# One TensorE program of FFT mixing and sorted experts: its order made by a count of every instruction

## The chip, the core and the metric

The kernel runs on one core of a Trainium2 chip. A core has a matrix engine (TensorE, PE in the profile; its weight loads are PEld), a vector engine (VectorE, DVE), a scalar engine (ScalarE, ACT), a general engine (GpSimd, POOL) and a queue processor that starts transfers (SyncE, SP). Each works through its own list of instructions in order and waits on semaphores for the others. Sixteen DMA engines move data. The metric is the time of one execution on the device in microseconds; the median of a few runs is compared.

## What is computed

The input `x` is 8 x 2496 x 256. Each channel of each batch goes through a Fourier transform along the sequence, a product with a learned filter, and the inverse transform. The result, seen as 19968 rows of 256, goes through a mixture of eight experts in which each row takes the one expert of largest logit.

```python
def _attn_ref(x, filt_r, filt_i):
    X = np.fft.rfft(x, axis=1)
    F = (filt_r + 1j * filt_i)[None, :, :]
    return np.fft.irfft(X * F, n=x.shape[1], axis=1).astype(np.float32)

def _moe_ref(x, w_gate, w1, w2):            # x (19968, 256), E = 8, F = 1024
    logits = x @ w_gate
    expert_idx = np.argmax(logits, axis=1)
    ...                                     # gate_w: softmax value of that expert
    for e in range(E):
        lo, hi = boundaries[e], boundaries[e + 1]      # rows sorted by expert
        h = np.maximum(x_sorted[lo:hi] @ w1[e], 0.0)
        y_sorted[lo:hi] = h @ w2[e]
    y = y_sorted[inv_perm]
    return gate_w[:, None] * y
```

## The kernel before

**The Fourier part.** 2496 is 39 x 64, and the transform is done in two short ones. For each batch: stage A multiplies blocks of `x` by the 39-point table (`tas`, L363), copies the result out of PSUM and stores it to DRAM (`zd`); stage B loads it the other way round (`fin<-zd`), multiplies by the 64-point table (`tbs`, L377), and VectorE multiplies by the filter in three instructions (L384 to L386) and adds two halves (on GpSimd in L390 or on VectorE in L393); stage C multiplies by the inverse table (`tcs`, L403), and its result is stored (`ud`); stage D loads that and multiplies by the last table (`tds`, L424). Batch 0 does the two turns in SBUF with transposes instead of DRAM (`first_a`, `turn_z`, `first_c`, `turn_u`). After stage D the rows are transposed, the logits are multiplied out (`logits` and `turn_logits` for batches 0 to 2, `block_logits` and `block_back` from batch 3), and `route` works out the expert and the row's place in the sorted list. GpSimd then scatters the rows to DRAM (`rows`, L693).

**The experts.** Sorted rows are read back in tiles of 512, 256 or 128 (`xg`), transposed on VectorE (L826), and multiplied by half of an expert's first weights at a time (`w1t`). Large tiles use a product of seven instead of eight blocks (`hidden_by_quarters`): GpSimd makes sums of blocks of `x` and `w1` (`sums`, `wsum`), VectorE adds the products together (L873), ScalarE takes the Relu (L877). Then each group of 128 rows is multiplied by the second weights (`w2t`, eight instructions of 128x256, L927), scaled by its gate (L931 or L932), and scattered to the output by GpSimd (L933).

**What sets the order.** The lists of TensorE, VectorE, ScalarE and SyncE are in the order in which the Python program emits instructions; GpSimd's list is arranged by the framework. The program keeps a list of Fourier steps, `STEPS`, sorted by hand-given places, each a tuple of place, function, load that it needs, assumed TensorE time, and chain ("a", "b", "d", "l"). A generator `experts()` yields the experts' pieces in their order. The main loop picks a Fourier step or an expert piece. It goes by a rough clock, `now[0]`, which grows by the assumed time of each step emitted, and by `free`, which holds rough times at which VectorE, ScalarE and GpSimd are done. A load is taken to land 7 to 13 us after it was asked for:

```python
lands[kind, b, c] = now[0] + (13.0 if kind != "x" and c < 2 else 10.0)
```

A step whose load is taken to be late is put off for another of the next sixteen; the steps that need another engine's output are placed by their place in the list alone. `credit` and `share()` mix expert pieces into the Fourier steps by the ratio of work left. `either` puts a copy out of PSUM on VectorE or ScalarE, whichever `free` says is done first.

Stores are kept in `moves` and issued by `flush` one round of the loop after they were asked for. `more_loads` asks for the next loads into seven `fin` buffers, and for `z` and `u` only after the stores of the whole batch are issued (`stored`). `prefetch` asks for rows and weights of coming expert tiles. `side` advances `route` by small pieces.

Of the kernel before, what the change touches and what calls it, by code (L numbers as in the profile page):

```python
# [19 lines left out]
P = 128  # L20
# [103 lines left out]

@with_exitstack
def kernel(
# [16 lines left out]
    nc = tc.nc  # L143
    mm = nc.tensor.matmul
    B = x.shape[0]
# [18 lines left out]
    dram = ctx.enter_context(tc.tile_pool(name="dram", bufs=1, space=DRAM))  # L164
# [7 lines left out]
    perm = ctx.enter_context(tc.tile_pool(name="perm", bufs=1))  # L172
# [9 lines left out]
    ps = ctx.enter_context(tc.tile_pool(name="ps", bufs=7, space=PSUM))  # L182

    fft = ctx.enter_context(ExitStack())
    cst = fft.enter_context(tc.tile_pool(name="cst", bufs=1))
    sb = fft.enter_context(tc.tile_pool(name="sb", bufs=2))
    psr = fft.enter_context(tc.tile_pool(name="psr", bufs=1, space=PSUM))
# [25 lines left out]
    pro = first.enter_context(tc.tile_pool(name="pro", bufs=2, side="right"))  # L213
# [4 lines left out]
    def experts_pool():  # L218
        first.close()
        pools["moe"] = ctx.enter_context(tc.tile_pool(name="moe", bufs=2, side="right", reuse_waits="tile"))  # L220
# [5 lines left out]
    now = [0.0]  # L226
    free = {"v": 0.0, "s": 0.0, "p": 0.0}

    def either(n, on_vector, on_scalar):

        v = max(free["v"], now[0]) + 0.15 + n / 960
        s = max(free["s"], now[0]) + 0.16 + n / 1200
        if v <= s:
            free["v"] = v
            on_vector()
        else:
            free["s"] = s
            on_scalar()

    def evac(o, i, n):  # L240
        either(n, lambda: nc.vector.tensor_copy(o, i), lambda: nc.scalar.copy(out=o, in_=i))

    def pool(start, n):

        free["p"] = max(free["p"], start) + 1.3 * n
        return free["p"]
# [36 lines left out]
    def make_constants():  # L283
        make_identity(nc, ident)
# [31 lines left out]
    ins, outs, lgs, yts, lands = {}, {}, {}, {}, {}  # L316
    NIN, YB = 7, 6

    moves, stored = [[], []], set()

    def move(o, i):
        moves[1].append(lambda: nc.sync.dma_start(out=o, in_=i))

    def mark(key):
        moves[1].append(lambda: stored.add(key))

    def flush(everything=False):
        for k in range(2 if everything else 1):
            for m in moves[k]:
                m()  # L330
        moves[:] = [[], []] if everything else [moves[1], []]
# [38 lines left out]
    def stage_b(b, f):  # L370
# [16 lines left out]
        free["v"] = max(free["v"], now[0]) + 2.1  # L387

        if b == 0 or b < 3 and not sides:
            nc.gpsimd.tensor_tensor(ys, ys, yw, op=ALU.add)  # L390
            free["p"] = max(free["p"], free["v"]) + (1.4 if b else 0.0)
        else:
            nc.vector.tensor_tensor(ys, ys, yw, op=ALU.add)  # L393
            free["v"] += 0.7
# [60 lines left out]
    def turn_z(f):  # L455
        if f % 4 == 0:
            nc.scalar.copy(out=ht[HP:, f:f + 4], in_=ht[:HP, f:f + 4])
            free["s"] = max(free["s"], now[0]) + 1.1
# [7 lines left out]
    def first_c(f):  # L466
# [6 lines left out]
        for h in range(DH):  # L473
            evac(zu["u"][:, h, :, :, f:f + 2], p[:, h].rearrange("p i c t -> p t c i"), D)

# [17 lines left out]
    def turn_y(b, c):  # L493
# [3 lines left out]
        if by_blocks(b):  # L497
# [3 lines left out]
            free["v"] = max(free["v"], now[0]) + 0.1 + n * D / 960  # L501
# [10 lines left out]

    turned_at = {}

    def turn_block(b, c):
        turn_y(b, c)
        turned_at["t", b, c] = max(now[0] + 4.0, free["v"] + 2.0)
# [4 lines left out]
    def block_logits(b, c):  # L522
# [10 lines left out]
        turned_at["s", b, c] = max(now[0], free["v"], free["s"]) + 1.5  # L533
# [35 lines left out]
    def route(b, c0, c1):  # L569
# [37 lines left out]
        due = free["v"] + 1.0  # L607
        while now[0] < due:
            yield "wait"
# [9 lines left out]
        free["s"] = max(free["s"], now[0]) + 1.2  # L619
# [15 lines left out]
        if by_blocks(b):  # L635
# [6 lines left out]
            due = free["v"] + 1.0  # L642
            while now[0] < due:
                yield "wait"
# [7 lines left out]
            free["s"] = max(free["s"], now[0]) + 0.3  # L652
# [12 lines left out]
        free["p"] = max(free["p"], now[0]) + 0.5 * len(yos)  # L665
        rows = []
        for t in range(w):
            m = N1 if t0 + t == NG - 1 else TP
            rows.append((row[:m, t:t + 1], yos[t // 4][:m, t % 4, :]))
        pool(now[0] + 2.0, 0)  # L670
        for t, (at, what) in enumerate(rows):
            scatter(b, at, what)
            yield "pool"
            if t % 4 == 3 or t == w - 1:
                held_y[0] -= 1
        if t0 + w == NG:
            rows_at[b] = free["p"] + 4.0
# [14 lines left out]
    def scatter(key, at, what):  # L692
# [11 lines left out]
        pool(now[0], 1)  # L704
# [117 lines left out]
    def turn_x(i):  # L822
# [4 lines left out]
        free["v"] = max(free["v"], now[0]) + DH * (0.15 + n * P / 960)  # L827
        if quarters(i):

            b = xts[i][:, :, :n * P].rearrange("p h (r c) -> p h r c", r=2)  # L830
            t = sums[i] = pools["moe"].tile([P, 3, 2 * P], F32, tag="sums", name="sums", bufs=2)[:, :, :n * HP]
            nc.gpsimd.tensor_tensor(t[:, 0], b[:, 0, 1], b[:, 0, 0], op=ALU.subtract)
            nc.gpsimd.tensor_tensor(t[:, 1], b[:, 1, 1], t[:, 0], op=ALU.subtract)

            nc.gpsimd.tensor_tensor(b[:, 0, 1], b[:, 1, 1], b[:, 0, 1], op=ALU.subtract)
            nc.gpsimd.tensor_tensor(t[:, 2], b[:, 1, 0], t[:, 1], op=ALU.subtract)
            free["p"] = max(free["p"], free["v"]) + 0.75 * n
            when["sums", i] = free["p"] + 1.0

    def w1_sums(h):  # L840

        w = w1t[h]
        t = wsum[h] = pools["moe"].tile([P, 3, 2 * P], F32, tag="wsum", name="wsum", bufs=2)
        nc.gpsimd.tensor_tensor(t[:, 0], w[:, 0, 1], w[:, 1, 1], op=ALU.add)  # L844
        nc.gpsimd.tensor_tensor(t[:, 1], t[:, 0], w[:, 0, 0], op=ALU.subtract)  # L845

        nc.gpsimd.tensor_tensor(w[:, 0, 1], w[:, 0, 0], w[:, 0, 1], op=ALU.subtract)
        nc.gpsimd.tensor_tensor(t[:, 2], w[:, 1, 0], t[:, 1], op=ALU.subtract)
        free["p"] = max(free["p"], now[0]) + 3.0
        when["wsum", h] = free["p"] + 1.0  # L850

    def hidden_by_quarters(h):
# [6 lines left out]
        w, ws, t = w1t[h], wsum[h], sums[i]  # L859
# [12 lines left out]
        def add(o, q, a):  # L872
            nc.vector.tensor_tensor(o, q, a, op=ALU.add)  # L873
            free["v"] = max(free["v"], now[0], free["s"] if o is first else 0.0) + 0.15 + 0.14 * n

        def relu(o, q):
            nc.scalar.activation(o.rearrange("p v r c -> p v (r c)"), q.rearrange("p v r c -> p v (r c)"), AF.Relu)  # L877
            free["s"] = max(free["s"], now[0], free["v"]) + 0.2 + 0.22 * n
# [4 lines left out]
        free["s"] = max(free["s"], now[0]) + 0.6  # L883
# [3 lines left out]
        q = product(ws[:, 1], t[:, 1])  # L887
# [4 lines left out]
        q = product(ws[:, 0], t[:, 0])  # L892
        add(hT[:, 1, :, 1], q, low)
        add(part, q, part)
        q = product(w[:, 1, 1], t[:, 2])
# [8 lines left out]
    def hidden(i, g, a):  # L904
# [10 lines left out]
        either(m, lambda: nc.vector.tensor_scalar_max(hT, p[:, :m], 0.0),  # L915
               lambda: nc.scalar.activation(hT, p[:, :m], AF.Relu))  # L916

    def result(i, j):
# [11 lines left out]
        pool(now[0], 1)  # L930
        either(D, lambda: nc.vector.tensor_scalar(ys, in0=p[:, :D], scalar1=gate, scalar2=None, op0=ALU.mult),  # L931
# [13 lines left out]
    def slot(k):  # L945

        steps, nch = [], len(CH)
        if k == 0:
            steps.append((0.4, load_rest, None, 0.0, None))
            for f in range(-2, NF + 2, 2):  # L950
                at = (f + 2) / (NF + 4)
                if 0 <= f < NF:
                    steps.append((at, lambda f=f: stage_b(k, f), None, 0.85, "b"))
                if f + 2 < NF:
                    steps.append((at + 0.01, lambda f=f: turn_z(f + 2), None, 0.44, "b"))
                if f >= 2:
                    steps.append((at + 0.02, lambda f=f: first_c(f - 2), None, 0.85, "b"))
        elif k < B:
            for f in range(0, NF + 4, 2):
                at = f / (NF + 4)  # L960
                if f < NF:
                    steps.append((at, lambda f=f: stage_b(k, f), ("z", k, f // 4) if f % 4 == 0 else None, 0.85, "b"))
                if f >= 4:
                    steps.append((at + 0.01, lambda f=f: stage_c(k, f - 4), None, 0.85, "b"))
# [277 lines left out]
```

## Time and profile before

| What | Value |
|---|---|
| Median of three runs | 1531.31 us (1528.97 to 1533.0) |
| The profiled execution | 1526.13 us, its span 1524.1 us |
| Mean granted TensorE clock | 0.992 |
| TensorE busy | 1458.8 us |
| VectorE, ScalarE, GpSimd busy | 769.3, 474.0, 698.2 us |
| Transfers | 276.89 MB, mean 182 GB/s |

In the profile a row of a group names line, engine, operation and tiles (output<-inputs), how often it ran, its busy time and the mean time of one. A row of waits names the engine and line that waited, what released it, and the total, number and longest of these waits in microseconds. A row of a stretch gives, after its bounds and length, the busy time and number of instructions of each engine, the granted clock as a share of full speed, the mean share of time in which the DMA engines were busy, and the GB/s moved. An SPq row is the queue processor's own wait or issue. A matrix instruction in fp32 leaves two records on PE.

### The profile page before, as it was taken

The page shows a single profiled execution, that of the slowest core. Times are in us where ns is not written, and L with a number is a line of the kernel's source. Part 1 is how long each engine was busy: PE and PEld are TensorE (multiplying, and loading weights), DVE is VectorE, ACT ScalarE, POOL GpSimd, SP SyncE. Part 2 cuts the span into 40 slices and gives each one's busy share as a digit, 9 for nine tenths or more (in the row PEclk, how much of TensorE's full clock was granted, in tenths as well). Part 3 has the DMA queues.
Part 4 walks back from the last instruction along what each step waited for, and adds up shares of the span by engine and source line. Part 5 has one row for each costly group of instructions (what it writes and reads, how often), then busy time and mean ns, then how long its engine had stood idle before and what let it go on. Part 6 is the DMA issues. An engine that isn't in the chain of part 4 may idle for free. (4 is left out here: it accounts for less than half of the span.)

```text
span 1524.1 us, 24305 instructions
## 1 busy us (share of the span) xinstructions
PE 1458.8 (96%) x7392; PEld 1147.9 (75%) x7392; DVE 769.3 (50%) x1712; ACT 474.0 (31%) x1003; POOL 698.2 (46%) x924
## 2 busy tenths in 40 slices
PE   7988897999988999999999999998999999999998
PEld 6543554776755866777778778887888889999997
DVE  4677585316665556567666565455525343440000
ACT  3444351233233233322232322222222222224332
POOL 4243334415523655545464556663545555741111
PEclk9999999999999999999999999999999999999999
DMA  9669898796479648657543744544566453455661
GB/s 241 196 180 313 250 321 244 213 250 224 135 208 273 182 129 251 186 170 186 172 133 112 210 113 126 159 132 128 163 169 192 142 175 102 123 185 170 185 186 39
DMA packets 216276, 276.89 MB, mean 182 GB/s; under 512 B 125209, under 2 KB 163610, under 8 KB 216147
## 3 DMA queue, kind: packets, MB, share of 16 engines
q1 hardware_dynamic: 197027, 231.99, 53.7%
q0 software_dynamic: 19120, 43.33, 8.3%
q8 instruction: 62, 1.02, 0.3%
q14 instruction: 67, 0.55, 0.1%
HBM read 195.24 MB, written 80.64 MB: 181 GB/s over the span
## 5 line engine op out<-in xcount | busy, mean ns | idle before, releaser
L927 PE MATMUL bank<-w2t,hT 128*128 128x256 f32 x1984 | 446.0, 383 | 8.3 <-ACT hT L877 7.8
L873 DVE TENSOR_TENSOR hT<-bank,hT 128x512 f32<-128x512 f32 (+1 forms) x504 | 298.7, 626 | 280.0 <-PE bank L869 188.0
L927 PEld LDWEIGHTS bank<-w2t,hT 128*128 128x128 f32 x1984 | 377.5, 191 | 70.6 <-issue 8.8
L933 POOL DMA_INDIRECT out_dram<-ys,ng x161 | 160.2, 995 | 451.2 <-ACT ys L932 111.7
L877 ACT ACTIVATE hT<-hT 128x1024 f32<-128x1024 f32 (+1 forms) x144 | 131.7, 955 | 345.4 <-DVE hT L873 345.2
L693 POOL DMA_INDIRECT rows<-yo,row x176 | 177.8, 1010 | 64.1 <-issue 44.2
L869 PE MATMUL bank<-xT,w1t 128*128 128x256 f32 (+1 forms) x864 | 191.6, 358 | 0.9 <-DVE yw L386 0.7
L932 ACT ACTIVATE ys<-bank,ng 128x256 f32<-128x256 f32 x135 | 63.8, 473 | 393.6 <-PE bank L927 325.8
L869 PEld LDWEIGHTS bank<-xT,w1t 128*128 128x128 f32 x864 | 152.2, 191 | 24.9 <-issue 5.7
L869 PE MATMUL bank<-sums,wsum 128*128 128x256 f32 (+1 forms) x576 | 137.3, 361 | 8.8 <-POOL wsum L845 4.3
L927 PE MATMUL bank<-w2s,hT 128*128 x592 | 132.6, 379 | 0.0
L826 DVE STREAM_TRANSPOSE xT<-xg 128x512 f32<-128x512 f32 (+2 forms) x126 | 57.4, 493 | 145.7 <-PE bank L910 119.6
L910 PE MATMUL bank<-xT,w1t 128*128 128x128 f32 (+1 forms) x864 | 123.4, 299 | 2.2 <-DVE xT L826 1.9
L869 PEld LDWEIGHTS bank<-sums,wsum 128*128 128x128 f32 x576 | 101.0, 191 | 28.8 <-issue 11.3
L910 PEld LDWEIGHTS bank<-xT,w1t 128*128 128x128 f32 x864 | 114.2, 191 | 11.1 <-issue 5.2
L927 PEld LDWEIGHTS bank<-w2s,hT 128*128 128x128 f32 x592 | 110.3, 190 | 13.8
L844 POOL TENSOR_TENSOR wsum<-w1t 128x256 f32<-128x256 f32 x72 | 52.9, 734 | 68.1 <-PE bank L869 65.9
L384 DVE TENSOR_TENSOR ys<-bank,ht 128x512 f32<-128x512 f32 x80 | 54.9, 687 | 55.5 <-PE bank L377 55.1
L403 PE MATMUL bank<-ys,tcs 128*128 128x512 f32 x140 | 73.7, 613 | 7.5 <-DVE ys L393 4.9
L363 PE MATMUL bank<-fin,tas 117*120 117x512 f32 x154 | 75.6, 610 | 5.4 <-DMA fin<-in_x_dram 4.5
L916 ACT ACTIVATE hT<-bank 128x128 f32<-128x128 f32 (+1 forms) x207 | 61.8, 299 | 48.1 <-PE bank L910 43.0
L377 PE MATMUL bank<-fin,tbs 128*128 128x512 f32 x140 | 72.6, 605 | 3.1 <-DMA fin<-zd 1.8
(160 smaller groups left out, 1602.1 us busy)
## 6 DMA issues: line engine op xcount, KB each, us to landing
w1t<-in_moe_w_dram SPq DMA_DIRECT2D x126, 512.0 KB
w2t<-in_moe_w_dram SPq DMA_DIRECT2D x68, 512.0 KB
fin<-in_x_dram SPq DMA_DIRECT2D x39, 512.0 KB
fin<-zd SPq DMA_DIRECT2D x70, 256.0 KB
ud<-uo SPq DMA_DIRECT2D x70, 256.0 KB
zd<-zo SPq DMA_DIRECT2D x35, 480.0 KB
fin<-ud SPq DMA_DIRECT2D x35, 480.0 KB
xg<-rows SPq DMA_DIRECT2D x112, 128.0 KB
```

The lines of the kernel that those rows point to most:

```text
L363: mm(p[:TK, :], lhsT=tas, rhs=xt[:TP, j:j + 2, :], start=True, stop=True)
L377: mm(p, lhsT=tbs, rhs=zi[:, j:j + 2, :], start=True, stop=True)
L403: mm(p, lhsT=tcs, rhs=ys, start=True, stop=True)
L693: sc = nc.gpsimd.indirect_dma_start(out=rowsd, out_offset=bass.IndirectOffsetOnAxis(ap=at, axis=0), in_=what, in_offset=None,)
L869: mm(q[:, v], lhsT=left[:, v * P:(v + 1) * P], rhs=right, start=True, stop=True)
L873: nc.vector.tensor_tensor(o, q, a, op=ALU.add)
L877: nc.scalar.activation(o.rearrange("p v r c -> p v (r c)"), q.rearrange("p v r c -> p v (r c)"), AF.Relu)
L910: mm(p[:, :m], lhsT=w1t[2 * i + g][:, dh, fh, v * P:(v + 1) * P], rhs=xts[i][:, dh, :m], start=(dh == 0), stop=(dh == DH - 1))
L916: lambda: nc.scalar.activation(hT, p[:, :m], AF.Relu))
L927: mm(p[:, :D], lhsT=hs[i][k % 4 // 2][:, k // 4, k % 2, j * P:(j + 1) * P], rhs=w2, start=(k == 0), stop=(k == FT - 1))
L932: lambda: nc.scalar.activation(ys, p[:, :D], AF.Copy, scale=gate))
L933: nc.gpsimd.indirect_dma_start(out=out, out_offset=bass.IndirectOffsetOnAxis(ap=gis[i].bitcast(U32)[:, j, :1], axis=0), in_=ys, in_offset= ...
```

## The change

The assumed times of steps and loads are replaced by a count. A class `Order` stands in front of the framework's engines. Every instruction that the program emits goes through it and is given a start: the latest of its engine's time, the counted end of its operands, and the counted release of the buffer that it writes (its last user `n` buffers ago). Its duration comes from a formula by engine and size. Transfers go through one counted stream. Matrix instructions that start over 1.2 us after the last one ended are counted at double time for 3.4 us.

```diff
+class Order:
+    HOP = 0.1
+    LOAD = 2.0
...
+    def transfer(self, out, in_):
+        n = min(self.run(out), self.run(in_), 4096)
+        packet = float(np.interp(n, (32, 64, 256, 1024, 4096), (9, 11, 18, 46, 159)))
+        size = 4 * int(np.prod([d[1] for d in in_.ap]))
+        return size / n * packet / 16e3
+
+    def count(self, engine, op, args, named):
...
+        kept = [a for a in ins if a.space != DRAM or a.name[:2] in ("zd", "ud")]
+        free = self.t[engine]
+        start = max([free] + [self.done.get(a.name, 0.0) + (self.HOP if engine != "sync" else 0.0) for a in kept])
+        if out is not None:
+            start = max(start, self.ahead.pop(out.name, 0.0))
...
+        if op.endswith("dma_start"):
+            busy = 1.0 if engine == "gpsimd" else 0.4
+            self.t[engine] = start + busy
+            took = self.transfer(out, named["in_"])
+            self.t["transfers"] = max(self.t["transfers"], start + busy) + took
+            end, tail = self.t["transfers"], self.LOAD
+        else:
...
+            elif engine == "tensor":
+                if start > self.busy + 1.2:
+                    self.slow = start + 3.4
+                rows = out.ap[0][1]
+                took = max(0.1, 0.00085 * n) if op == "transpose" else max(0.216, 0.00169 * n) if rows > 32 else 0.00045 * n
+                took *= 2.0 if start < self.slow else 1.0
+                tail = 0.25
+            elif engine == "vector":
+                took = 0.15 + n / 960
+            elif engine == "scalar":
+                took = 0.16 + n / 1200
+            else:
+                took = 0.06 + n / 375
```

`either` now also looks at the counted end of its input. The add of stage B goes to GpSimd when that is counted to cost little, not by batch:

```diff
-        if b == 0 or b < 3 and not sides:
+        if max(t["gpsimd"], t["vector"]) + 1.43 <= t["vector"] + (1.5 if b < 3 else 0.7):
             nc.gpsimd.tensor_tensor(ys, ys, yw, op=ALU.add)
         else:
             nc.vector.tensor_tensor(ys, ys, yw, op=ALU.add)
```

Stores go, in order, when their source is counted ready:

```diff
-    def flush(everything=False):
-        for k in range(2 if everything else 1):
-            for m in moves[k]:
-                m()
-        moves[:] = [[], []] if everything else [moves[1], []]
+    def flush():
+        while moves and (moves[0][0] is None or nc.ready(moves[0][0]) <= t["tensor"] + 0.2):
+            moves.pop(0)[1]()
```

Each Fourier step gains a sixth entry, the tiles that it reads; `turn_block` and the chain of `turned_at` go, and their steps read `yts` and `outs["s", ...]` in the same way. Two examples:

```diff
-                    steps.append((at, lambda f=f: stage_b(k, f), None, 0.85, "b"))
+                    steps.append((at, lambda f=f: stage_b(k, f), None, 0.85, "b", lambda f=f: [outs["zi", f]]))
...
-                    steps.append((at, lambda c=c: stage_d(k - 1, c), ("u", k - 1, c) if k > 1 else "y", 0.43 * CH[c][1], "d"))
+                    steps.append((at, lambda c=c: stage_d(k - 1, c), ("u", k - 1, c) if k > 1 else "y", 0.43 * CH[c][1], "d",
+                                  lambda c=c: [ins["u", k - 1, c] if k > 1 else outs["ui", c]]))
```

For an expert piece `when` gives the counted time of its tiles: rows, weights, sums, or the hidden layer and second weights. The main loop takes the first candidate that is counted ready within 0.2 us; when none is, it moves TensorE's counted time on:

```diff
+            steps = list(open_steps())
+            choice = [(f, wait_of(f)) for f in steps]
+            if known:
+                late_by = max(0.0, when(e[2]) - t["tensor"])
+                choice.insert(0 if credit > 0.0 or not fs else 1, (e, late_by))
+            choice = [c for c in choice if c[1] is not None]
+            pick, late_by = next((c for c in choice if c[1] <= 0.2), min(choice, key=lambda c: c[1]) if choice else (None, 0.5))
+            if late_by > 0.2:
+                t["tensor"] += min(late_by, 0.5)
+            elif pick is e:
                 e[0]()
-                now[0] += e[1]
                 credit -= e[1]
                 e = next(es, None)
-            elif f and ready(fs[n]):
-                f = fs.pop(n)
-                f[1]()
-                now[0] += f[3]
-                credit = (credit if asked else 0.0) + share() * f[3]
-                left_t[0] -= f[3]
             else:
-                now[0] += 1.0
+                fs.remove(pick)
+                pick[1]()
+                credit = (credit if known else 0.0) + share() * pick[3]
+                left_t[0] -= pick[3]
```

`open_steps` gives the first step of each chain among the next sixteen. The same clock replaces `now[0]` in `prefetch`, `side`, `route` and `due`. Arithmetic, tiles, buffers and the loads' sizes are as before.

## What was predicted before the changed kernel ran

> **What bounds the kernel now.** I read the page's busy times first, then the stretches of 100 us, then TensorE's waits, then the SP queue's waits, and last two places in the timeline.
>
> ```profile
> span 1524.1 us, 24305 instructions
> PE 1458.8 (96%) x7392; PEld 1147.9 (75%) x7392; DVE 769.3 (50%) x1712; ACT 474.0 (31%) x1003; POOL 698.2 (46%) x924
> ```
>
> TensorE is busy for 96% of the span, and the change neither adds nor removes a matmul. All it can win is TensorE's idle time, 1524.1 - 1458.8 = 65.3 us, and time at a lowered clock. The stretches (PE, PEld, DVE, ACT, POOL busy, then granted clock, DMA share, GB/s) say where that lies:
>
> ```profile
> 0.00:100.00 100.00, 86.92 (x440) 56.33 (x441) 57.23 (x109) 44.31 (x87) 37.86 (x57) 1.00 0.74 202
> 100.00:200.00 100.00, 88.65 (x329) 46.45 (x328) 66.36 (x167) 38.45 (x90) 39.35 (x49) 0.98 0.88 280
> 200.00:300.00 100.00, 87.24 (x372) 57.73 (x371) 60.28 (x181) 33.06 (x76) 41.08 (x58) 0.97 0.86 258
> 300.00:400.00 100.00, 99.88 (x485) 74.27 (x486) 44.07 (x97) 32.08 (x74) 40.65 (x54) 1.00 0.75 221
> 400.00:500.00 100.00, 91.46 (x420) 63.36 (x411) 59.30 (x133) 31.27 (x62) 39.07 (x53) 0.97 0.75 204
> 500.00:600.00 100.00, 95.69 (x454) 71.45 (x453) 60.28 (x117) 30.88 (x58) 57.81 (x76) 0.98 0.67 197
> 1000.00:1100.00 100.00, 96.14 (x444) 83.70 (x443) 52.45 (x120) 23.93 (x34) 51.01 (x67) 1.00 0.50 148
> ```
>
> Idle: 13.1 us in the first 100, 11.4 + 12.8 = 24.1 in the next 200, about 21.4 from 300 to 1100 (0.1, 8.5, 4.3, and 8.5 after 600), nothing from 1100 to 1500, 6.5 at the end. The clock shares 0.98, 0.97, 0.97, 0.98 are 2 + 3 + 3 + 2 = 10 us lost at half clock, half of it before 300. From 100 to 300 the transfers are the second limit: share 0.88 and 0.86.
>
> ```profile
> PE bank L927 <- ACT hT L877: 7.8, 2, 4.3
> PE bank L869 <- DVE hT L873: 5.9, 5, 2.0
> PE bank L446 <- DMA fin<-in_x_dram: 5.1, 2, 4.2
> PE bank L403 <- DVE ys L393: 4.9, 3, 1.7
> PE bank L363 <- DMA fin<-in_x_dram: 4.5, 2, 3.9
> PE bank L869 <- POOL wsum L845: 4.3, 1, 4.3
> ```
>
> Each row is who waited, who released it, total us, times, longest. Most are matmuls put too close behind the engine that makes their operand; two rows are loads.
>
> ```profile
> 441.04 2.00 ACT L877 ACTIVATE hT<-hT 128x1024 f32<-128x1024 f32 x2 [4.34 <-DVE hT L873]
> 443.09 3.15 PE L927 MATMUL bank<-w2t,hT 128*128 128x256 f32 x7 [4.27 <-ACT hT L877]
> ```
>
> Here a result matmul stands right behind the last product of its hidden layer; the Relu ends 4.27 us later. With other work in between that wait is gone: this is what the change is about.
>
> **The change, part by part.** I weigh the order of TensorE's instructions, before and after, by the spacing of matmul starts in this trace (0.43 us for a 128x256 instruction, which is two records, 0.86 for 512 columns, 0.11 for a transpose); the whole order is 1412 us of such work in both. For each operand I then count the work between the matmul it descends from and the matmul that uses it.
>
> 1. *Pieces go when counted ready.* Distances that were zero or short grow: Relu output to first result matmul, shortest three 0.9, 4.0, 4.3 before and 4.0, 6.7, 6.9 after; `zi` to stage B, 0.0 before and 0.9 after; `ui` to stage D, 0.0 and 0.9; route's `oe` to its two matmuls, under 3 us in 7 of 24 cases before and 3 after. Operands used under 0.6 us after their engine's last matmul, whatever the engine: 12 before, 3 after. One grows worse: block_back's `ls` stands under 2 us behind block_logits in 13 of 30 cases, not 6. Its copy takes 0.27 us on ScalarE; at about 0.5 us for each of 7 more I book 4 us of loss (bounds 0 and 7 x 2).
>
> In the first 100 us, 4.2 of the idle 13.1 are the first load, which stays. Of the other 8.9 I take 5 (bounds 0 and 8.9). From 300 to 1100 the bounds are 0 and 21.4 + 5 of clock = 26; I take 14, nearer the top, because the long waits (4.3, 4.3, and the 2.0 and 1.7) stand where the distances grew, and free FFT pieces are at hand until work position 877.
>
> The clock row first: from 110 to 120 us the granted clock was 0.83 though the waits there (L403 above) were at most 1.7 us.
>
> ```profile
> 110.00:120.00 10.00, 6.73 (x12) 2.52 (x12) 4.93 (x8) 2.79 (x5) 6.66 (x7) 0.83 0.83 246
> ```
>
> The Trainium skill (TensorE: Matmul & The Clock Gate, What's actually happening) has the clock fall after a wholly idle window of some 3.4 us. By that page only the waits of about 4 us cost clock, some 7 of the 10 us, and by this row short waits in a cluster cost it too, so the whole 10 hangs on all of them; the measurement decides.
>
> 2. *Transfers and the SP queue.* Stores now leave when their source is counted ready, not one round later. What is behind a held store: later stores, the `stored` marks, and so the z and u loads. In the SP queue the loads already wait for stores to land:
>
> ```profile
> SPq L322 <- ACT zo L241: 74.1, 18, 16.6
> SPq L355 <- DMA ud<-uo: 25.4, 9, 5.7
> SPq L348 <- DMA zd<-zo: 22.6, 8, 6.7
> ```
>
> Such a wait also holds every load queued behind it, weights and x among them. By work position, the new order asks for 20.9 MB between 100 and 150 (18.2 before) and 18.0 between 150 and 225 (24.6 before); the first expert matmul moves from position 126 to 144, so there is less filler in the tight part. From 100 to 300 the transfers are busy 88 + 86 = 174 us, so at most 26 of those 200 us can go. At the 280 GB/s of the row 100:200, 20.9 MB need 75 us and 18.2 need 65: at worst 10 are lost. I take the middle of -10 and +26, a gain of 8, for idle time and clock of this stretch.
>
> 3. *Who does what.* 15 of the 65 adds L393 go from VectorE to GpSimd, 23 of the gate multiplies go from VectorE to ScalarE, 15 Relus the other way.
>
> ```profile
> L390 POOL TENSOR_TENSOR ys<-ys,yw x15: 1262/1272/1275, 24.3 to 158.4; 128x512 f32<-128x512 f32 x15
> L393 DVE TENSOR_TENSOR ys<-ys,yw x65: 691/693/1901, 87.2 to 844.5; 128x512 f32<-128x512 f32 x65
> ```
>
> Each moved add makes the chain B to C 1.27 - 0.69 = 0.58 us longer. It is hidden by other matmuls: the shortest B-to-C distances are 1.7, 2.6, 3.4 after and 1.7, 2.6, 2.7 before. I take 0; without that cover it is 15 x 0.58 = 9 us. Row first again: none of the 15 GpSimd adds is stretched (1262 to 1275), though one VectorE add took 1901. The Trainium skill (SBUF — State Buffer, SBUF: two separate sides) says that a GpSimd op that reads SBUF and a VectorE op with two SBUF inputs lock each other out for a whole instruction, which speaks against moving adds there. By that page 15 blocks of 1.27 us would add up to 19 us of VectorE time, by the row nearly none; VectorE, busy 66 of 100 us at most, has room for either.
>
> 4. *The tail.* From work position 900 on, TensorE's order is the same: no idle there from 1100 to 1500, nothing to win or lose.
>
> Sum: 5 + 14 + 8 - 4 = 23 us. The profiled execution's span of 1524.1 (time 1526.1) becomes 1501 (1503). The median of the runs, 1531.3, is 5 us above that execution; I take the same 23 from it: 1508.
>
> **Rivals.**
> - *Slower: transfers land later than counted.* The count has one stream of transfers, each landing 2 us after its turn, and no limit to how many are open; the SP queue shows stores taking up to 6.7 us to land before a load may start. After the change a dozen z, u and x loads between positions 85 and 140 stand only 9.6 to 14 us behind the matmul that their SP issue hangs on; before it was mostly 11 to 14, with one of 7.9 that cost no listed wait. If such loads come 3 us late on average: 12 x 3 = 36, and 6 spells at half clock at 1.7 each, 10: 46 against the 23, 1554. It decides from about 2 us of mean lateness (23 / 12). For it: the DMA share 0.88. Against it: the waits for loads were only some 11 us of 65 before, in the same dense stretch.
> - *No change: the waits only move.* Transfers bound everything up to 300, and the later gain (14) is eaten by `ls` (4), by adds on GpSimd (9): 1530. Against it: the stretches after 300 have DMA shares of 0.5 to 0.75.
> - *The count is not what runs on GpSimd.* GpSimd's instructions are not held to the program's order (94 places are out of order after, 109 before), so `wsum`, scatters and adds are counted wrongly. Then the wait for `wsum` (4.3) stays and some adds come late (half of 9): 23 - 8 = 15, 1516.
> - *Nearly all idle goes.* 8 + 17 + 20 - 2 = 43: 1488.
>
> **How the numbers follow.** Forecast about 1508 (own range 1494 to 1522) 0.45; nearly all 0.12; GpSimd's order 0.13; no change 0.10; slower 0.20. A measurement tells apart some 0.3%, 4.6 us. Faster is 0.45 + 0.12 + 0.13 = 0.70, same 0.10, slower 0.20. The range runs from 1488, with little left below it, to 1540, which takes in the beginning of the slower case.
>
> **What would show it.** Right: TensorE's idle below 15 us in 300 to 1100; no wait of L927 for `hT` above 2 us; the granted clock 0.99 or more after 300; DMA share above 0.9 from 100 to 250. Wrong: waits of stage B or D for `fin` from `zd` and `ud` of more than 20 us in total, more spells of half clock than before, or idle time in the tail.

## The result, and the profile after

The changed kernel takes 1538.4 us (median of 5 runs, 1536.45 to 1539.34), the kernel before beside it 1530.75 us: a ratio of 1.0051, 95% interval 1.0036 to 1.0067. It is slower by half a per cent, where 1508 us, faster, had been forecast. Two later comparisons gave 1.0070 (1.0052 to 1.0088) and 1.0045 (1.0030 to 1.0061). The profiled execution took 1536.45 us.

In the trace of after nearly every instruction goes through the wrapper of `Order`, so nearly all rows carry its line, L228; tiles and engines tell them apart. The page's span and busy times:

```profile
span 1534.7 us, 24323 instructions
PE 1460.6 (95%) x7392; PEld 1151.7 (75%) x7392; DVE 756.9 (49%) x1696; ACT 480.5 (31%) x1004; POOL 715.6 (47%) x939
```

TensorE is busy 1.8 us longer than before and idle 74.1 us, not 65.3. The stretches of after (PE, PEld, DVE, ACT, POOL busy, granted clock, DMA share, GB/s):

```profile
0.00:100.00 100.00, 88.58 (x446) 57.82 (x446) 52.85 (x101) 49.77 (x97) 40.34 (x59) 1.00 0.75 203
100.00:200.00 100.00, 74.98 (x249) 34.52 (x248) 55.18 (x130) 30.91 (x67) 40.00 (x46) 0.86 0.81 241
200.00:300.00 100.00, 81.51 (x347) 56.40 (x348) 56.76 (x167) 29.70 (x70) 44.86 (x61) 0.90 0.75 222
300.00:400.00 100.00, 100.00 (x478) 71.94 (x477) 44.26 (x121) 36.34 (x88) 38.82 (x50) 1.00 0.87 267
400.00:500.00 100.00, 95.76 (x423) 69.09 (x422) 63.41 (x121) 33.23 (x59) 48.79 (x67) 1.00 0.77 216
500.00:600.00 100.00, 100.00 (x508) 78.83 (x507) 61.29 (x126) 31.27 (x63) 56.37 (x74) 1.00 0.55 159
1000.00:1100.00 100.00, 100.00 (x465) 88.03 (x464) 52.41 (x121) 26.59 (x39) 56.00 (x74) 1.00 0.55 163
```

From 300 us on the change did what it was made for: the stretches at 400, 500 and 1000 us are 95.8, 100 and 100 us busy, not 91.5, 95.7 and 96.1. Over 300 to 1100 us idle fell from 21.4 to 12.5 us. Between 100 and 300 us it rose from 24.1 to 43.5 us, the clock fell from 0.98 and 0.97 to 0.86 and 0.90, and the DMA share fell too, so the transfers are no busier limit than before. With 1.7 us won in the first 100: 1.7 + 9.0 - 19.4 = -8.7 us, the growth of the idle time. TensorE's waits in after:

```profile
PE bank L228 <- POOL ys L228: 16.6, 4, 9.9
PE bank L228 <- POOL wsum L228: 10.7, 2, 7.2
PE bank L228 <- DMA fin<-in_x_dram: 9.1, 5, 4.1
PE bank L228 <- DVE oe L228: 7.7, 3, 6.2
PE bank L228 <- DVE ys L228: 6.3, 2, 6.0
PE bank L228 <- DMA fin<-zd: 2.1, 2, 1.5
PE bank L228 <- DMA fin<-ud: 0.7, 1, 0.7
```

The waits for the Relu's `hT` that headed the list before have gone. At the head stands GpSimd's `ys`, the add of stage B, 16.6 us in four waits, the longest 9.9 us. The timeline of after shows that one, first TensorE, then GpSimd (start, duration, instruction, in brackets idle time and releaser):

```profile
164.65 1.02 PE L228 MATMUL bank<-ys,tcs 128*128 128x512 f32 x2
175.54 2.93 PE L228 MATMUL bank<-ys,tcs 128*128 128x512 f32 x3 [9.87 <-POOL ys L228]
```

```profile
163.75 1.07 POOL L228 DMA_INDIRECT rows<-yo,row  x1 [1.67 <-DVE yt L228]
165.13 0.99 POOL L228 DMA_INDIRECT rows<-yo,row  x1 [0.30 <-issue]
166.42 0.99 POOL L228 DMA_INDIRECT rows<-yo,row  x1 [0.30 <-ACT uo L228]
...
170.30 0.90 POOL L228 DMA_INDIRECT rows<-yo,row  x1 [0.30 <-issue]
173.85 0.29 POOL L228 TENSOR_SCALAR yo<-ids 117x32 int32<-117x32 f32 x1 [2.65 <-DMA rows<-yo,row]
174.22 2.48 POOL L228 TENSOR_TENSOR ys<-ys,yw 128x512 f32<-128x512 f32 x2
```

VectorE had made both operands of the two adds by 165.7 and 167.9 us. They ran at 174.22, behind six scatters and behind a fill of `yo` that had itself to wait 2.65 us for a scatter to have read its buffer. A scatter follows the last at 1.29 us (0.99 busy, 0.30 issue). The add's own 1.27 us is the smallest part of the wait.

The matmul at 175.54 us waits for the first of these two adds, and that one is not among the 15 that changed engine: the kernel before issues it on GpSimd as well. There no scatter stood ahead of it, and it ran as soon as VectorE was done:

```profile
158.37 1.26 POOL L390 TENSOR_TENSOR ys<-ys,yw 128x512 f32<-128x512 f32 x1 [5.38 <-DVE yw L386]
```

So for the longest wait it was the new order that put scatters ahead of an add. Of the adds that changed engine, the one with the longest wait (5.45 us) ran at 140.37 us, behind five scatters:

```profile
139.36 0.99 POOL L228 DMA_INDIRECT rows<-yo,row  x1 [0.30 <-issue]
140.37 1.27 POOL L228 TENSOR_TENSOR ys<-ys,yw 128x512 f32<-128x512 f32 x1
```

### The profile page after: what moved, and what is told of

Same layout as the page of the kernel before. It is cut to its first block, busy times and chain, and to the rows that moved or that the text cites. A ratio compares the mean times of both kernels' runs of the same rounds, so it can differ in the third digit from the quotient of the medians.

```text
span 1534.7 us, 24323 instructions
## 1 busy us (share of the span) xinstructions
PE 1460.6 (95%) x7392; PEld 1151.7 (75%) x7392; DVE 756.9 (49%) x1696; ACT 480.5 (31%) x1004; POOL 715.6 (47%) x939
## 5 line engine op out<-in xcount | busy, mean ns | idle before, releaser
L228 DVE TENSOR_TENSOR hT<-bank,hT 128x512 f32<-128x512 f32 (+1 forms) x504 | 299.9, 627 | 315.7 <-PE bank L228 213.8
L228 PE MATMUL bank<-w2t,hT 128*128 128x256 f32 x1984 | 441.5, 380 | 0.4 <-ACT hT L228 0.4
L228 PEld LDWEIGHTS bank<-w2t,hT 128*128 128x128 f32 x1984 | 374.9, 190 | 60.4 <-issue 8.6
L228 POOL DMA_INDIRECT out_dram<-ys,ng x161 | 161.1, 1001 | 438.2 <-ACT ys L228 121.8
L228 PE MATMUL bank<-xT,w1t 128*128 128x256 f32 (+1 forms) x1728 | 320.2, 331 | 7.9 <-DMA w1t<-in_moe_w_dram 4.1
L228 PEld LDWEIGHTS bank<-xT,w1t 128*128 128x128 f32 x1728 | 268.9, 193 | 45.8 <-issue 16.0
L228 ACT ACTIVATE hT<-hT 128x1024 f32<-128x1024 f32 (+1 forms) x144 | 132.9, 957 | 347.5 <-DVE hT L228 347.3
L228 POOL DMA_INDIRECT rows<-yo,row x176 | 175.5, 997 | 61.3 <-issue 41.8
L228 ACT ACTIVATE ys<-bank,ng 128x256 f32<-128x256 f32 x157 | 74.1, 473 | 386.4 <-PE bank L228 345.4
L228 PE MATMUL bank<-sums,wsum 128*128 128x256 f32 (+1 forms) x576 | 136.4, 359 | 10.7 <-POOL wsum L228 10.7
L228 PE MATMUL bank<-w2s,hT 128*128 x592 | 132.6, 379 | 0.0
L228 PEld LDWEIGHTS bank<-sums,wsum 128*128 128x128 f32 x576 | 101.6, 191 | 28.4 <-POOL wsum L228 11.2
L228 PEld LDWEIGHTS bank<-w2s,hT 128*128 128x128 f32 x592 | 110.3, 190 | 13.8
L228 PE MATMUL bank<-ys,tcs 128*128 128x512 f32 x140 | 76.5, 633 | 21.7 <-POOL ys L228 15.3
L228 DVE TENSOR_TENSOR ys<-bank,ht 128x512 f32<-128x512 f32 x80 | 54.9, 687 | 62.4 <-PE bank L228 62.1
L228 POOL TENSOR_TENSOR wsum<-w1t 128x256 f32<-128x256 f32 x72 | 53.3, 740 | 65.0 <-PE bank L228 55.8
L228 PE MATMUL bank<-fin,tas 117*120 117x512 f32 x154 | 75.7, 612 | 4.1 <-DMA fin<-in_x_dram 4.1
L228 PE MATMUL bank<-fin,tds 120*128 120x512 f32 (+1 forms) x168 | 77.4, 581 | 0.7 <-DMA fin<-ud 0.7
L228 PE MATMUL bank<-fin,tbs 128*128 128x512 f32 x140 | 72.7, 605 | 2.1 <-DMA fin<-zd 2.1
L228 PE MATMUL bank<-xT,wsum 128*128 128x256 f32 (+1 forms) x288 | 69.0, 362 | 3.5 <-DVE hT L228 2.4
L228 ACT ACTIVATE hT<-bank 128x128 f32<-128x128 f32 (+1 forms) x186 | 56.3, 302 | 49.4 <-PE bank L228 37.8
L228 DVE STREAM_TRANSPOSE xT<-xg 128x512 f32<-128x512 f32 (+2 forms) x126 | 57.5, 495 | 27.7 <-PE bank L228 12.4
```

What stands on the lines that cost most here:

```text
L228: return real(*args, **named)
```

## The experiments

Two theories. Theory Q: the adds moved to GpSimd queue behind its scatters. Theory T: the count lets work stand on transfers that land later than counted, and the adds only show it. Later came Theory C: the luck of one order. The kernel before took 1530 to 1532 us on the chips of the result and of the y, z and last batches, and 1555 to 1559 us on those of the x and of the h and w1 batches. So ratios are compared within a kind of chip; below, "first kind" and "second kind".

### The rule of the add, and the transfers (second kind, kernel before 1554.8 us)

x1 takes the old rule for the add, all else counted. x2 counts a transfer's source as released only once it has landed. x4 adds slower transfers and issues to x2, x5 is x1 and x4 together.

```diff
# x1
-        if max(t["gpsimd"], t["vector"]) + 1.43 <= t["vector"] + (1.5 if b < 3 else 0.7):
+        if b == 0 or b < 3 and not sides:
# x2
-    LOAD = 2.0
+    LOAD = 4.0
-            self.used[a.name] = max(self.used.get(a.name, 0.0), end)
+            self.used[a.name] = max(self.used.get(a.name, 0.0), end + tail * op.endswith("dma_start"))
# x4: x2 and
-        return size / n * packet / 16e3
+        return size / n * packet / 16e3 * 1.35
-            busy = 1.0 if engine == "gpsimd" else 0.4
+            busy = 1.3 if engine == "gpsimd" else 0.55
```

> The changed kernel with one part undone: the add of stage B goes to GpSimd by the rule of before (batch 0, or batches 1 and 2 while no route is under way), else to VectorE. Theory Q (the moved adds queue behind scatters on GpSimd): the 16.6 us of TensorE's waits for GpSimd's ys and most of the half clock around them go, 1538 - 20 = 1518. Theory T (the count lets transfers land too early, and everything between 100 and 300 us that hangs on them is late, the adds too): the waits move to another engine, 1530 to 1538, and the idle time from 100 to 300 stays above 35 us.

> The changed kernel with a stored buffer counted free when its store has landed, and a landing counted at 4 us after the transfer, not 2. Theory T: the 12 us in which VectorE stood at 110 to 121 us before a buffer whose store was under way, and the 6.2 us wait for oe, go; 1538 - 10 = 1528. Theory Q: within 0.3% of the changed kernel, 1534 to 1542, because the adds stay behind the scatters.

> As x2_release, and the count's transfers take 1.35 times as long, an issue 0.55 us on SyncE and 1.3 on GpSimd (the spacing of scatters in the trace is 1.29). The adds may still go to GpSimd. Theory T: the count no longer runs ahead of the chip between 100 and 300 us, idle there falls from 43.5 to below 25, 1515. Theory Q: the adds still stand behind scatters, 1530 or more, with over 10 us of TensorE's waits for GpSimd's ys.

> x1_adds_rule and x4_slow_transfers together. Theory Q: as x1_adds_rule, 1518. Theory T: as x4_slow_transfers, 1515. If the two losses are separate and add up: 1505.

Measured: x1 1531.2 us, 0.9847 (0.9817 to 0.9877); x2 1535.0, 0.9876 (0.9849 to 0.9902); x4 1557.3, 1.0007 (0.9992 to 1.0023); x5 1551.1, 0.9971 (0.9945 to 0.9998). Counting all transfers slower makes the kernel slower by 20 us: the waits are not bought off by caution everywhere, since the experts then come late (idle of 12.4 us between 500 and 600 us in x4, none in after). In x1 TensorE's waits for GpSimd's `ys` are 1.3 us, in x2 5.0. Theory T missed: in x2 the wait for `oe` did not go but grew to 15.3 us, x4 stands 42 us above that theory's 1515 us, and x5 33 us and more above what either theory gave it. But the changed kernel was not in this batch, so the size of x1's gain was open.

### Only the adds, with the order kept (first kind, kernel before 1532.4 us)

Two orders drawn up by different rules differ in about a third of the rows of TensorE's list, so x1 changed more than the adds. y1 keeps the changed kernel's order: the 15 adds are still counted as GpSimd's, but issued on VectorE. y2 does the reverse to the kernel before. y0 is the changed kernel, y3 the changed kernel with another semaphore hop, `HOP = 0.15`, which alters the order alone.

```diff
# y1, in the changed kernel; moved = the 15 (b, f) of batches 1 and 2
-            nc.gpsimd.tensor_tensor(ys, ys, yw, op=ALU.add)
+            nc.count("gpsimd", "tensor_tensor", (ys, ys, yw), {})
+            on = nc.nc.vector if (b, f) in moved else nc.nc.gpsimd
+            on.tensor_tensor(ys, ys, yw, op=ALU.add)
# y2, in the kernel before, L393
-            nc.vector.tensor_tensor(ys, ys, yw, op=ALU.add)
+            on = nc.gpsimd if (b, f) in moved else nc.vector
+            on.tensor_tensor(ys, ys, yw, op=ALU.add)
```

> The changed kernel itself beside the kernel before, on the chip of this batch. Both theories: ratio to before 1.003 to 1.007, as at first (1.0051), if the two chips price the waits alike. If on this chip it is below 1.00 while the kernel before is 1.5% slower than at first, then the earlier batch's ratios below 1 said more of the chip than of their edits, and only differences to this run count. TensorE's waits for GpSimd's ys: 16 us in about 4.

> The order of the changed kernel kept to the last instruction (the 15 adds of batches 1 and 2 are still counted as GpSimd's), but those 15 adds are issued on VectorE at the same place. Theory Q (the adds queue behind the scatters on GpSimd, and that is the loss): TensorE's waits for GpSimd's ys fall from 16.6 us to under 3, the time falls by 12 to 20 us against the changed kernel (half-clock time after the long waits included). Theory T (the order is drawn up for transfers that land too early, the adds only show it): the waits go to loads, oe and VectorE's ys instead, and the time falls by less than 5 us. VectorE's queue gains 15 x 0.58 = 9 us between 115 and 280 us in both.

> The kernel before with its order kept, but with the same 15 adds of batches 1 and 2 issued on GpSimd. Theory Q: GpSimd's scatters hold these adds here too; new waits for ys of 8 to 16 us in 100 to 300 us, and the time rises by 8 to 18 us against the kernel before. Theory T: the order of before leaves room, TensorE's waits for ys stay under 4 us and the time rises by less than 4 us.

> The changed kernel with a semaphore's hop counted at 0.15 us and not 0.10: no cost that the traces show is met better or worse, only the order comes out differently in places. Both theories Q and T: within 5 us of the changed kernel, with 12 to 20 us of waits for ys between 100 and 300 us. If chance in the order is what decides (Theory C: where a scatter or a load falls before a step is luck), it differs from the changed kernel by 8 us or more in either direction.

Measured: y0 1542.8 us, 1.0070; y1 1533.0, 1.0001 (0.9991 to 1.0011); y2 1542.5, 1.0062 (1.0040 to 1.0085); y3 1534.1, 1.0009 (0.9995 to 1.0023). The 15 adds cost 9.8 us in the one order (1542.8 - 1533.0) and 10.2 us in the other (1542.5 - 1532.4). That is as near a proof as such a kernel gives: the same 15 instructions, moved both ways, and in the traces the lists of TensorE, VectorE, ScalarE and GpSimd are the same but for these adds. TensorE at the same two instructions in y0, then in y1:

```profile
142.74 2.08 PE L228 MATMUL bank<-ys,tcs 128*128 128x512 f32 x2 [6.01 <-POOL ys L228]
174.98 2.93 PE L228 MATMUL bank<-ys,tcs 128*128 128x512 f32 x3 [8.85 <-POOL ys L228]
```

```profile
137.29 1.10 PE L228 MATMUL bank<-ys,tcs 128*128 128x512 f32 x2 [0.65 <-DVE ys L507]
168.12 3.58 PE L228 MATMUL bank<-ys,tcs 128*128 128x512 f32 x4 [9.46 <-POOL ys L507]
```

The wait of the moved add has gone; that of the unmoved one, the longest of the result's trace, stays, which is why y1's expectation (12 to 20 us, waits under 3 us) was too high. y2 met its own: 8 to 18 us, with 12.4 us of waits for `ys`. The place fits too, though not all of the size: compared at the same instruction of TensorE's list, y0 is 6.2 us behind y1 at about 300 us and y2 10.8 us behind the kernel before. What these pairs of single executions differ by later (3.3 and 7.3 us) arose where no moved add is, and is not explained.

y2 shows what else such an add holds. In the kernel before with the adds moved, first GpSimd, then VectorE, then TensorE:

```profile
113.78 0.99 POOL L695 DMA_INDIRECT rows<-yo,row  x1 [0.30 <-issue]
115.07 0.99 POOL L695 DMA_INDIRECT rows<-yo,row  x1 [0.30 <-issue]
116.09 1.26 POOL L395 TENSOR_TENSOR ys<-ys,yw 128x512 f32<-128x512 f32 x1
```

```profile
113.17 0.69 DVE L384 TENSOR_TENSOR ys<-bank,ht 128x512 f32<-128x512 f32 x1
117.39 0.69 DVE L385 SCALAR_TENSOR_TENSOR yw<-bank,ht 64x512 f32<-64x512 f32 x1 [3.52 <-POOL ys L395]
```

```profile
117.41 2.07 PE L405 MATMUL bank<-ys,tcs 128*128 128x512 f32 x2 [7.08 <-POOL ys L395]
122.47 2.07 PE L405 MATMUL bank<-ys,tcs 128*128 128x512 f32 x2 [2.99 <-POOL ys L395]
```

There are only two `yw` buffers: the late add holds one, so VectorE stands still for 3.52 us with all of its list behind it.

y3 met Theory C's number (8 us or more): a hop that matches no wait moved the time by 8.8 us, though TensorE still waited 14.1 us for GpSimd's `ys`. So the order's luck alone can be as large as the price of the 15 adds, and Theory C has a share in everything that changes the order.

### All adds on VectorE, and the count's releases (first kind, kernel before 1530.2 us)

z1 is y1 with every add from batch 1 on issued on VectorE: five more than in y1, not the three that its expectation names. z2 is x1 once more. z3 is x1 with x2's release line (not its `LOAD`). z5 is z3 with all adds from batch 1 on both counted and issued on VectorE.

```diff
# z1
+            on = nc.nc.vector if b else nc.nc.gpsimd
# z5
-        if b == 0 or b < 3 and not sides:
+        if b == 0:
```

> The changed kernel's order kept once more, with every add of batches 1 and later issued on VectorE (y1 still had three of them on GpSimd, one of which made TensorE wait 9.5 us). Theory Q: the waits for GpSimd's ys after 100 us are gone (10.8 us in y1, 16.4 in the changed kernel), and the time is 6 to 12 us under y1's, that is 16 to 22 us under the changed kernel (1.007 of before), so 0.993 to 0.997 of before. Theory T: the waits come back at oe, w1t, ys of VectorE and wsum; the time stays within 4 us of y1's (1.000 of before).

> x1_adds_rule once more (the count decides all but the add, which goes by the rule of before), since the kernel before was 1.5% slower on the chip of x1 than on the other two. If the ratio carries from chip to chip: 0.982 to 0.988. If it was that chip that slowed the kernel before alone: 1525 to 1535 us and a ratio of 0.995 to 1.002; then the gain over the changed kernel (1.007) is 8 to 18 us, Theory Q's 12 to 20 with the change of order in it.

> x1 with the second repair: the source of a transfer counts as released when the transfer has landed (its end and the 2 us behind it), not when its last byte is counted. Waits for oe, which stood behind a copy into a store's buffer that was not yet free (9.1 us in x1, 7.4 in the changed kernel), fall under 4 us. If so and nothing replaces them, 5 to 10 us under z2_rule_again. If the order's chance decides, anything from 8 us less to 8 us more.

> As z3, but every add of batches 1 and later on VectorE, and counted there. Theory Q: GpSimd's ys never holds TensorE after 100 us; VectorE's queue is longer by 0.58 us for each of the adds that the rule of before gives to GpSimd between routes (some 5): within 3 us of z3. Waits for VectorE's ys may grow from 6 to 10 us; above that, VectorE is the bound here and z5 is slower than z3.

Measured: z1 1528.1 us, 0.9982 (0.9968 to 0.9995); z2 1512.0, 0.9894 (0.9868 to 0.9921); z3 1516.6, 0.9902 (0.9866 to 0.9937); z5 1514.6, 0.9906 (0.9883 to 0.9930). The adds on VectorE in the kept order bring the changed kernel 0.2% below the kernel before, less than expected (0.993 to 0.997): a wait of 9.8 us for a copy of `yo` on VectorE took the place of the add. Where the count knows that the adds are VectorE's (z2, z3, z5), it is 1.0% faster than before; z2's ratio lies between the two ranges that its expectation gave. The repaired release (z3) adds nothing: `oe` still costs 10.0 us, in z2 11.7. VectorE's timeline in z2 says why:

```profile
216.41 0.15 DVE L228 TENSOR_TENSOR done<-done,take 1x8 f32<-1x8 f32 x1
226.57 1.31 DVE L228 STREAM_TRANSPOSE xT<-xg 128x512 f32<-128x512 f32 x2 [10.01 <-DMA xg<-rows]
...
232.62 0.39 DVE L228 TENSOR_TENSOR oe<-idx,em 117x64 f32<-117x64 f32 x1
```

VectorE stood 10.01 us at a transpose of sorted rows that had not landed, with a filter product and all of `route` behind it, `oe` last. The same holds in z1: there VectorE waits 8.89 us at such a transpose, and the copy of `yo` is behind it.

### The luck of the order, and rows counted later (second kind, kernel before 1558.9 us)

h1 is the changed kernel with a hop of 0.12 us, h2 and h3 are z2 with 0.05 and 0.15. w1 is z2 with only the rows' loads counted later:

```diff
-            end, tail = self.t["transfers"], self.LOAD
+            end, tail = self.t["transfers"], self.LOAD + (6.0 if named["in_"].name.startswith("rows") else 0.0)
```

> The changed kernel with a hop counted at 0.12 us. Three orders of the changed kernel's rule are then known: 0.10 us (1.005 and 1.007 of before), 0.15 us (1.001) and this one. Theory Q: 1.000 to 1.010, since the adds go to GpSimd ahead of or behind the same scatters. Theory C (luck of the order): anywhere from 0.985 to 1.015.

> z2_rule_again (the count, with the add rule of before) with a hop counted at 0.05 us. Theory Q: 0.985 to 0.995 of before, near z2's 0.9894, and below every order of the changed kernel's rule. Theory C: the spread of the two rules overlaps, this one may stand at 1.00.

> The same with 0.15 us. Theory Q: 0.985 to 0.995 of before. Theory C: anywhere from 0.98 to 1.01; three orders of one rule that lie more than 15 us apart would leave the size of the rule's effect open.

> z2_rule_again, with loads of sorted rows (xg) counted as landing 8 us after their counted end in place of 2: VectorE stood 8 to 10 us at a transpose of xg in three of the traces, and everything in its list behind that (oe, ys, a copy out of PSUM) held TensorE 5 to 11 us. If that is what is left between 100 and 300 us, the wait for oe at 221 us (11.0 us) goes, half-clock time of 17 us there falls to under 7, and the time is 8 to 15 us under z2_rule_again. If the margin only delays the experts (as all slower transfers together did in x4), the time rises and idle comes after 500 us.

Measured: h1 1543.3 us, 0.9900 (0.9871 to 0.9930); h2 1528.5, 0.9813 (0.9783 to 0.9843); h3 1535.7, 0.9858 (0.9828 to 0.9888); w1 1512.6, 0.9705 (0.9675 to 0.9735). On the first kind the changed kernel's rule gave 1.0009 to 1.0070 (y0, y3, y5 and the result), the old rule, or VectorE where the count knows it, 0.9894 to 0.9906 (z2, z3, z5); on the second kind 0.9900 against 0.9813 to 0.9858. No median of one group lies inside the other, though the intervals of h1 and h3 touch. With hops for noise the rule of the add is worth 0.4 to 1.8%; 10 us (0.6%) is what the kept order gave for the queue, the rest can't be told from the order's luck, which is some 4 us either way (h2, x1 and h3: 1528.5, 1531.2, 1535.7). Taken as written, h1 (1.000 to 1.010) and h2 (0.985 to 0.995) lie below Theory Q's ranges and h3 inside its own; these ranges came from ratios on the first kind, and h2 and h3 are read here against h1. Theory C had allowed h1 and h3 as well. w1 is 18.6 us under x1, more than the 8 to 15 us expected.

### The best order beside the changed kernel (first kind, kernel before 1532.1 us)

> The changed kernel itself, beside w3. On a chip like the first, the fourth and the fifth (kernel before 1530 to 1532 us): 1.003 to 1.009 of before. On a chip like the two on which the kernel before took 1555 to 1559 us, with engines held up for nothing that the profile shows: 0.985 to 0.995, near h1's 0.990.

> w1_rows_late once more, beside the changed kernel. If the margin on the rows is worth what w1 showed on its chip (1.2% under x1 on a like chip), then on a chip where the kernel before takes 1530 to 1532 us it stands at 0.975 to 0.985 (1493 to 1509 us); if that was the luck of one order on one chip, 0.985 to 0.995. In both it is below the changed kernel by 15 us or more.

y5 is the changed kernel: 1539.2 us, 1.0045 (1.0030 to 1.0061). w3 is w1: 1496.7 us, 0.9765 (0.9741 to 0.9788), 42.5 us below it and 2.35% below the kernel before. TensorE's waits in w3:

```profile
PE bank L228 <- DMA fin<-in_x_dram: 17.7, 8, 7.4
PE bank L228 <- DMA fin<-ud: 7.2, 4, 3.2
PE bank L228 <- DVE ys L228: 3.7, 1, 3.7
...
PE bank L228 <- POOL wsum L228: 1.7, 1, 1.7
PE bank L228 <- POOL ys L228: 1.3, 2, 1.0
```

`oe` is gone from the list, as w1's expectation had it, and most of what is left are loads of x and `ud`. Six microseconds for the one kind of load that VectorE stands under won 15 us (1512.0 to 1496.7; on the second kind 1531.2 to 1512.6), where slower transfers and issues throughout lost 22 (x2 to x4). Both times the order changed too; that both kinds of chip give 1.3 to 1.4% (ratios of 0.9894 and 0.9765, 0.9847 and 0.9705) speaks against luck of the chip, not against luck of the order.

## Why the prediction was wrong

**Part 1 (5 in the first 100 us, 14 from 300 on): right in kind and nearly in size.** 1.7 us in the first 100. From 300 to 1100 us 9.0 us of idle went, and half-clock time fell from three spells of 3.4 us to one, worth some 3.4 us: 12.4 against 14. That is one execution; in the traces of y0 and y5, the same kernel, idle over this stretch is 14.7 and 12.9 us, and half-clock time is no shorter than in the kernel before. The sign to look for (idle under 15 us, no wait of the result matmuls for `hT` over 2 us, clock 0.99 after 300 us) came true; the DMA share above 0.9 from 100 us on did not.

**Part 3 (the 15 adds: "It is hidden by other matmuls", 0): this is the step that failed first.** It priced an instruction by its duration, 1.27 against 0.69 us, and its cover by the work on TensorE between stages B and C. It never asked what stands ahead of the add in GpSimd's own list. There stand scatters at 1.29 us each, up to six or eight in a row, and a fill that waits for a scatter. The uncovered price of 9 us had the right size by accident: what was measured, 10 us in both directions, comes with a few long waits (6.0 us in y0; 7.1 and 3.0 us among the four of y2) and not with 15 times 0.58. Of the 30 us between the 1508 forecast and the 1538.4 measured, these adds are 10. Most of the rest lies in the stretch of part 2; no run that keeps the order isolated it.

**Part 2 (transfers and SP's queue, +8 of -10 to +26): wrong in sign, and not by its own mechanism.** The stretch lost 19.4 us of idle. The feared waits for `zd` and `ud` came to 2.8 us, and the DMA share fell. What the part left out is that a load need not hold TensorE itself: VectorE stands at a buffer or at rows, and what is behind it in its list holds TensorE. The timeline of after at the first such place:

```profile
108.75 0.68 DVE L228 TENSOR_TENSOR yw<-bank,ht 64x512 f32<-64x512 f32 x1
121.50 1.29 DVE L228 COPY zo<-bank 120x512 f32<-120x512 f32 x2 [12.07 <-DMA ud<-uo]
...
123.86 0.23 DVE L228 TENSOR_TENSOR oe<-idx,em 117x64 f32<-117x64 f32 x1
```

VectorE waits 12.07 us for a store to have left the buffer that `zo` gets; `oe` is behind it and holds TensorE 6.2 us. What stands behind such a wait decides: the kernel before has one of 15.5 us at 250 us and w3 one of 9.5 us at 122 us, and in neither did TensorE wait for `oe` more than 0.6 us in all. The count releases a store's source without the 2 us that it gives every landing. Set against the trace, the count of the changed kernel has TensorE's instruction of 84 us within 2.3 us and that of 284 us 41 us too early, in jumps at `oe`, GpSimd's `ys` twice, `w1t`, VectorE's `ys` and `wsum`; up to 1000 us it then stays 40 to 51 us too early. Its own end for TensorE, 1507.8 us, is near the forecast's figure, but partly by luck: both left out the same queues, while after 1000 us the chip is faster than the count and makes up some 20 us.

**`ls` (-4): nothing.** No wait for `ls` is in the list of after.

**The clock.** The six waits of 4.1 us and more between 100 and 300 us (6.2, 5.4, 9.9, 4.1, 6.0, 7.2) each brought 6.8 or 10.2 us at half clock, the one of 2.6 us none: 48 us in all, of which TensorE was idle for 19. Its busy time over the whole rose by 1.8 us only; why not by more is not shown. The Trainium skill (TensorE: Matmul & The Clock Gate, What's actually happening) ties the fall to a wholly idle window of some 3.4 us. These rows agree with it. Two others do not, and stand unexplained: the row of before with 0.83 and waits of 1.7 us at most, and in after 3.4 us at half clock at 819 us, behind a wait of 2.4 us.

**The rivals.** "No change" (1530 us) came nearest in number, and of its three reasons one held, the adds on GpSimd (9 us; 10 measured); `ls` cost nothing, and the first 300 us did not stay as they were but lost 17.7 us of idle. The slower one was right in sign and wrong in place: transfers do land later than counted, but at buffers and rows on VectorE, not at `zd` and `ud`. "The count is not what runs on GpSimd" named the place and had it as a smaller gain: the fill in the GpSimd rows above stands ahead of two adds that were ready. That fill by itself, and a scatter counted at its 1.29 us and not 1.0, were not tried. Without the moved adds the sum comes nearly true: z2 took 1512.0 us, the forecast being 1508. But it does not come true by its parts: between 100 and 300 us z2 is idle for 29.9 us, more than the 24.1 of before, where part 2 had a gain of 8. That makes the nearness part luck, and z2's order is another as well.

## What to carry to other kernels

An instruction moved to another engine costs what stands ahead of it in that engine's list, not its duration; look for runs of transfers issued by that engine. To price a step, keep the order and move that step alone, in both kernels: the two answers agreed to 0.4 us here, while a reordering by a count moves the time by 9 us for no cause that the traces show. Where a scheduler counts, try first to correct the one transfer that an in-order engine stands under: here that won 15 us, in an order that changed with it, and slowing all of them lost 22.

## What the runs showed of the hardware

The same kernel took 1512.0 us on a chip of the first kind (z2) and 1531.2 us on one of the second (x1). Matrix instructions last the same in both (379 ns for 128x256). What differs are waits for nothing that the profile shows. In z2 ScalarE has 38.0 us of these, VectorE and TensorE none; in x1 80.9, 18.0 and 4.0 us. The largest such row of each of these engines, in z2, then in x1:

```profile
ACT ys L228 <- issue: 31.9, 10, 4.8
```

```profile
ACT ys L228 <- issue: 59.2, 19, 4.8
DVE lg L228 <- issue: 13.2, 1, 13.2
PE bank L228 <- issue: 4.0, 4, 1.7
```

The cause was not tried. The kernel before loses more there (1.6 to 1.9%) than x1 does (1.3%); why was not tried either, so the sign of a half per cent can turn with the chip: h1, the changed kernel in all but a hop, is at 0.990 there.

In after three small VectorE instructions, `rs<-rs` of 117x6 or 117x8, took about 1.0 us longer than their usual 0.17 us, each beside a GpSimd add. The Trainium skill (SBUF — State Buffer, SBUF: two separate sides) has a VectorE instruction in a two-port mode, or with two SBUF inputs, and a GpSimd one lock each other out for the whole instruction; which of the two cases these three are, no run shows. Three such blocks, 3.0 us in all, is what this trace shows of the 19 us that a block for each moved add would have made.
